# Two first loads change queues, and block 1's raw transposes go ahead of V of block 0

## The chip, the cores and the metric

The kernel runs on one core of a Trainium2 chip. A core has TensorE (PE, matrix products), VectorE (DVE), ScalarE (ACT), GpSimd (POOL) and SyncE (SP), which work side by side and wait for one another through semaphores. Loads and stores are DMAs; here SyncE, ScalarE and GpSimd issue them, each in its own queue, and the core's 16 DMA engines carry them out. The metric is the device time of one execution in microseconds (us).

## What is computed

The input x is 2048 rows of 512, in bfloat16. The result is the sum of x and two branches that both read the row-normalised x:

```python
xn = _layernorm(x, axis=-1)
return x + _A_ref(xn, A_wqkv, A_wo) + _B_ref(xn, B_w_in, B_w_sp, B_b_sp, B_w_out)
```

Branch A is attention with 32 heads of 16. Row s looks at the eight rows s, s-2, ..., s-14; Q, K and V come from one weight matrix of 512 x 1536, and a 512 x 512 matrix follows. Branch B multiplies xn by a 512 x 1792 matrix and takes GELU. It normalises the second half of the columns (z2), mixes it over all 2048 rows by a 2048 x 2048 matrix, adds a bias for each row, multiplies by the first half (z1), and projects back to 512 columns.

## The kernel before

**Tiling.** The rows are cut into 16 blocks of 128. Every matrix product needs x with the features on the partitions, so each block is transposed. Blocks 0 to 2 (`NRAW = 3`) are transposed raw by TensorE, against an identity matrix (`pe_tr`, L600): four matmuls of 128 columns a block, named xTx0a and xTx0b (two each), xTx1 and xTx2. ScalarE copies these from PSUM to SBUF (L628: xTc0_0, xTc0_1, xTc1_0, xTc1_1, xTc2_0). The product V of these blocks is made from the raw transposes, four matmuls of 512 columns a block, in two halves (V0_0, V0_1 and so on, L700). Each half reads the half of V's weights that it needs: `wv` half 0 (loaded by ldwv0) and half 1 (ldwv1), 256 KB each. Mean and scale are put right later. Beside this VectorE takes the statistics of each block (L620, L622, L632), GpSimd the inverse root (L634) and VectorE normalises (L646). Block 0's normalised rows are transposed by TensorE (xTr0, also L600, copied by ScalarE in L608), those of the later blocks by DMA (L640, named xTd1 and on, issued by SyncE). z2 is L831, Q and K are L723, z1 is L877, the mixing over rows L977, the two output products L1033 and L1042.

**Order.** Each operation is a task with engine, estimated time, reads and writes. `Plan.schedule` simulates the engines in the program's own time and fixes one static order for each engine; it uses estimates, and for some DMAs a landing time given in `land`. The eight banks of PSUM are given out as the simulation goes. Lists of names in `build_kernel` add edges that force an order; the longest is that of TensorE's first work. `Plan.emit` writes each engine's instructions with the waits that the order needs. An engine works strictly in its order, so an instruction that waits holds up all behind it.

**The first loads.** x of block b is 128 KB (`ld_x`, L535; ldx0 is written out in L562). ScalarE's queue issues ldx0 and ldx1 and then loads its activation table. SyncE's queue issues ldwv0, ldwv1, ldx2, ldx3, the two halves of z2's weights and more rows of x.

**The warm-up.** While nothing has landed, TensorE multiplies constants (`warm`, L581): warm0 to warm5 with 512 columns, warm6 with 128, and one more, warm7, with 128 columns, behind block 0's raw transposes.

Of the kernel before, what the change touches and what calls it, by code (L numbers as in the profile page):

```python
# [346 lines left out]
def build_kernel(nc, A_x, A_wqkv, A_wo, B_x, B_w_in, B_w_sp, B_b_sp, B_w_out, out, report=False, emit=True):  # L347
# [13 lines left out]
    NWARM = 7  # L361
# [8 lines left out]
    off = {}  # L370
# [40 lines left out]
    with ExitStack() as es:  # L411
# [5 lines left out]
        def A(name, n, o2_=0):  # L417
            return ar[:, off[name] + o2_: off[name] + o2_ + n]

        def AC(o_, dims):  # L420
            return bass.AP(tensor=ar, offset=o_, ap=[[AR, 128]] + [list(d) for d in dims])
# [10 lines left out]
        def P(bk, n, o_=0):  # L432
            return ps[:, bk.col(o_): bk.col(o_) + n]
# [78 lines left out]
        def dma(eng, fn, nbytes, chan, reads=(), writes=(), name="", xbar=False, prio=0.0, after=()):  # L512
            return T(eng, fn, reads=reads, writes=writes, name=name, prio=prio, after=after,
                     dma=dict(chan=chan, nbytes=nbytes, xbar=xbar, iss=(1270.0 if nbytes < 400000 else 2200.0) if xbar else None))
# [18 lines left out]
        def ld_x(b, eng="sp"):  # L533
            sl = b
            return dma(eng, lambda e: e.dma_start(A("xin", 512, 512 * sl), x2[128 * b:128 * b + 128, :]), 128 * 512 * 2,  # L535
                ("xin", sl), writes=[("xin", sl)], name="ldx%d" % b)

        def ld_wv(hf):
            dma("sp", lambda e: e.dma_start(AC(off["wv"] + 1024 * hf, [[512, 2], [1, 512]]),
                                            A_wqkv[256 * hf:256 * hf + 256, 1024:1536].rearrange("(c p) n -> p c n",  # L540
                                                                                               p=128)),
                256 * 512 * 2, ("wv", hf), writes=[("wv", hf)], name="ldwv%d" % hf)
# [13 lines left out]
        def ld_wqk(which, eng):  # L556
# [4 lines left out]

        dma("act", lambda e: e.dma_start(A("xin", 512), x2[0:128, :]), 128 * 512 * 2, ("xin", 0),  # L562
            writes=[("xin0", 0), ("xin0", 1)], name="ldx0")
        ld_x(1, "act")
        ld_wv(0)
        ld_wv(1)
        ld_x(2, "sp")
        ld_x(3, "sp")
        ld_win2a()
# [6 lines left out]
        ld_wqk(1, "sp")  # L576

        bw = plan.bank("warm")
        for wi in range(NWARM + 1):
            n_ = 512 if wi < 6 else 128  # L580
            T("pe", (lambda bw, n_: lambda t: t.matmul(P(bw, n_), ones[:, 0:128], ones[:, 0:n_], start=True,  # L581
                                                       stop=True))(bw, n_),
              writes=[bw], est=(427.0 if n_ == 512 else 107.0), name="warm%d" % wi, prio=1000)
# [487 lines left out]

        byname = {t.name: t for t in plan.tasks}
        for names in (["warm%d" % wi for wi in range(NWARM)] +
                      ["xTx0a", "xTx0b", "warm%d" % NWARM, "V0_0", "xTx1", "V0_1", "xTx2", "V1_0", "V1_1", "xTr0", "V2_0", "V2_1",
                       "z2_0_0", "z2_0_0b", "z2_0_1", "z2_1_0", "z2_1_1", "z2_2_0", "z2_2_1", "V3_0", "V3_1", "z2_3_0", "z2_3_1", "V4_0", "V4_1", "z2_4_0", "z2_4_1", "Q0_0", "Q0_1", "K0_0", "K0_1"],
                      ("rstd7", "Vw3"),
                      ("bnst0", "bnag0", "vpe0", "bnst1", "bnag1", "vpe1", "norm0", "bnst2", "norm1", "bnag2", "vpe2", "bnst3", "norm2",
                       "bnag3", "vpe3", "norm3", "bnst4", "bnag4", "vpe4", "mr", "norm4", "bnst5"),
                      ["bnst%d" % b for b in range(5, NB)],
                      ("xTc0_0", "xTc0_1", "xTc1_0", "xTc1_1", "xTc2_0", "xTe0_0", "xTe0_2", "Ve1", "Ve0", "Ve2",  # L1080
                       "z2g0", "z2g1", "z2s0"), ("ldx4", "xTd1", "xTd2", "xTd3", "xTd4", "ldq", "ldk", "ldx5", "ldx6", "ldx7", "ldwin1", "ldx8"), ("ldx15", "xTd5"),
                      *[("ldwin1", "ldx%d" % b) for b in range(9, NB)], *[("z2_4_1", "%s0_%d" % (n, c)) for n in "QK" for c in range(4)],
                      ("V10_1", "Q3_3"), ("csa", "csb", "csc", "csr", "ldwout"), ("csr", "ldwo0"), ("csr", "ldxr0"), ("csv", "zr3")):
            for n0, n1 in zip(names, names[1:]):
                if byname[n0] not in byname[n1].deps:
                    byname[n1].odeps.add(byname[n0])

        plan.schedule(tol=4.0, dma_bw=285.0, dma_lat=1600.0, overlap=60.0,
                      land=dict(ldx0=3600.0, ldwv0=4120.0, ldx1=4550.0, ldwv1=5230.0, ldx2=5600.0, ldwin2a=7650.0, ldx3=6050.0,
                                ldwin2b=8950.0, csa=75800.0, csb=78400.0, csc=83400.0, csr=86500.0, ldx4=9100.0, ldx5=18150.0, ldq=16300.0, xTd3=12130.0, ldk=17800.0, ldx6=18500.0, ldx7=18900.0, xTd4=13900.0, xTd1=9600.0, xTd2=10850.0, ldwin1=21500.0))  # L1090
        if report:
            print("arena", AR, "fp", FR)
# [17 lines left out]
def bass_parallel_sum__sliding_local_dilated__mixer_gmlp__prompt_kernel(  # L1110
    nc, A_x, A_wqkv, A_wo, B_x, B_w_in, B_w_sp, B_b_sp, B_w_out, out
):
    build_kernel(nc, A_x, A_wqkv, A_wo, B_x, B_w_in, B_w_sp, B_b_sp, B_w_out, out)
# [28 lines left out]
```

## Time and profile before

| | |
|---|---|
| median of 3 runs | 236.63 us (235.77 to 236.96) |
| the profiled execution | 236.54 us |
| its span, first to last instruction | 235.3 us |
| TensorE busy | 232.4 us, 99% |
| VectorE busy | 207.3 us, 88% |
| ScalarE busy | 95.9 us, 41% |
| data moved by DMA | 44.55 MB, mean 189 GB/s |

The span leaves out 1.2 us of the profiled execution's time. A line of the timeline gives the start and the length in us from the span's start, the engine, the line of the kernel, the operation with its output and input, the shapes, how many instructions are merged, and in brackets how long the engine was idle before and what ended that. A queue is named by its engine with a q behind it (SPq, ACTq). Matmuls are pipelined, so a matmul's length holds its drain, and the distance between starts says how fast TensorE streams. A line of the DMA issues gives the issuing queue, the number, the size and the time from issue to landing.

### The profile page before, as it was taken

To read this page: it belongs to the slowest core of one execution; us is meant where nothing else is said; L and a number is where in the kernel's file an instruction comes from. 1 tells how busy PE (TensorE), PEld (TensorE's weight loads), DVE (VectorE), ACT (ScalarE), POOL (GpSimd) and SP (SyncE) were. 2 spreads that over 40 slices of the span, in tenths; PEclk is the share of its full clock that TensorE was granted. 3 is DMA by queue.
4 is the path that set the end of the run, shared out by engine and by line. 5 is a ranking of instruction groups with operands and counts; after the bars stand their busy time and mean duration, and the time that the engine had idled before them with its cause. 6 is when DMAs were issued, how large, how long until landed. Compare 5 with 4: busy or idle time off the path is not lost.

```text
span 235.3 us, 3002 instructions
## 1 busy us (share of the span) xinstructions
PE 232.4 (99%) x1127; PEld 109.0 (46%) x1127; DVE 207.3 (88%) x271; ACT 95.9 (41%) x143; POOL 29.4 (12%) x58
## 2 busy tenths in 40 slices
PE   8999999999999999999999999999999999999996
PEld 3545445544454444444444444444444444444443
DVE  4706899999999999999899999998899998999723
ACT  3788878888986679610120531111111111000000
POOL 2305740404361202000000000000000000000000
PEclk9999999999999999999999999999999999999999
DMA  6669934999911285346199999999969849945442
GB/s 221 203 193 368 181 68 103 215 202 214 228 45 50 67 231 173 66 94 175 58 353 239 273 212 266 195 236 288 279 180 306 269 145 303 288 115 156 111 137 68
DMA packets 83991, 44.55 MB, mean 189 GB/s; under 512 B 56180, under 2 KB 83204, under 8 KB 83976
## 3 DMA queue, kind: packets, MB, share of 16 engines
q1 hardware_dynamic: 82744, 41.94, 69.6%
q0 software_dynamic: 800, 2.11, 3.0%
q10 hardware_dynamic: 432, 0.30, 0.4%
q8 instruction: 9, 0.15, 0.3%
q14 instruction: 6, 0.05, 0.1%
HBM read 26.62 MB, written 4.22 MB: 131 GB/s over the span
## 4 chain that ended last, share of the span: by engine, by line
PE 98%; DVE 0%; ACT 0%; issue 0%; DVEq 0%
PE ps L977 41%; PE ps L723 12%; PE ps L831 10%; PE ps L877 10%; PE ps L1042 10%; PE ps L700 6%; PE ps L1033 6%; PE ps L581 1%; PE ps L767 1%; PE ps L600 1%; DVE arena L1048 0%; ACT arena L628 0%; PE ps L778 0%; DVEq L325 0%
## 5 line engine op out<-in xcount | busy, mean ns | idle before, releaser
L977 PE MATMUL ps<-arena 128*128 128x512 bf16 x448 | 97.0, 379 | 0.0
L977 PEld LDWEIGHTS ps<-arena 128*128 128x128 bf16 x448 | 43.8, 98 | 53.0 <-issue 0.4
L985 ACT ACTIVATE arena<-ps 128x1024 bf16<-128x1024 f32 (+1 forms) x16 | 14.7, 917 | 77.0 <-PE ps L977 70.6
L1005 DVE TENSOR_TENSOR arena<-arena 128x4096 bf16<-128x4096 bf16 x16 | 36.4, 2282 | 0.0
L744 DVE TENSOR_TENSOR arena<-arena 128x4096 bf16<-128x4096 bf16 x16 | 36.4, 2280 | 0.0
L1008 DVE TENSOR_TENSOR arena<-arena 128x2048 bf16<-128x2048 bf16 (+1 forms) x32 | 30.0, 948 | 0.2
L723 PE MATMUL ps<-arena 128*128 128x512 bf16 x128 | 28.8, 379 | 0.0
L749 DVE TENSOR_TENSOR arena<-arena 128x4096 bf16<-128x4096 bf16 x12 | 27.4, 2287 | 0.1
L1042 PE MATMUL ps<-arena 128*128 128x512 bf16 (+2 forms) x119 | 27.0, 366 | 0.0
L831 PE MATMUL ps<-arena 128*128 128x448 bf16 x128 | 25.5, 352 | 0.0
L877 PE MATMUL ps<-arena 128*128 128x512 bf16 x112 | 24.5, 379 | 0.0
L723 PEld LDWEIGHTS ps<-arena 128*128 128x128 bf16 x128 | 14.4, 113 | 13.3 <-ACT arena L713 0.4
L732 ACT ACTIVATE arena<-ps 128x1024 bf16<-128x1024 f32 x16 | 16.2, 1022 | 6.8 <-PE ps L723 6.6
L1048 DVE TENSOR_TENSOR arena<-ps,arena 128x512 bf16<-128x512 f32 (+2 forms) x17 | 11.2, 656 | 8.6 <-PE ps L1042 8.5
L831 PEld LDWEIGHTS ps<-arena 128*128 128x128 bf16 x128 | 12.5, 98 | 12.1 <-issue 0.2
L1042 PEld LDWEIGHTS ps<-arena 128*128 128x128 bf16 x119 | 11.4, 98 | 12.9
L877 PEld LDWEIGHTS ps<-arena 128*128 128x128 bf16 x112 | 11.0, 98 | 13.2
L700 PE MATMUL ps<-arena 128*128 128x512 bf16 x64 | 16.8, 395 | 0.2 <-ACT arena L628 0.2
L1033 PE MATMUL ps<-arena 128*128 128x512 bf16 (+2 forms) x68 | 16.6, 366 | 0.0
L839 ACT ACTIVATE arena<-ps 128x896 bf16<-128x896 f32 x16 | 14.6, 913 | 3.4 <-PE ps L831 3.3
L883 ACT ACTIVATE arena<-ps 128x1024 bf16<-128x1024 f32 (+1 forms) x16 | 14.0, 919 | 4.4 <-PE ps L877 4.3
L620 DVE BATCH_NORM_STATS2 fpool<-arena 128x6 f32<-128x512 bf16 x16 | 10.7, 685 | 5.5 <-DMA arena<-in_A_x_dram 5.5
(64 smaller groups left out, 168.2 us busy)
## 6 DMA issues: line engine op xcount, KB each, us to landing
arena<-vscr SPq DMA_DIRECT2D x16, 1024.0 KB, 6.1
arena<-in_A_x_dram SPq DMA_DIRECT2D x30, 128.0 KB, 3.8
vscr<-arena POOLq DMA_DIRECT2D x16, 128.0 KB, 3.9
out_dram<-arena SPq DMA_DIRECT2D x15, 128.0 KB, 2.0
arena<-in_A_wqkv_dram SPq DMA_DIRECT2D x2, 512.0 KB, 4.6
arena<-in_B_w_in_dram SPq DMA_DIRECT2D x2, 448.0 KB, 4.9
arena<-in_B_w_in_dram SPq DMA_DIRECT2D x1, 896.0 KB, 8.2
arena<-in_B_w_out_dram SPq DMA_DIRECT2D x1, 896.0 KB, 5.9
```

The source lines that it names most:

```text
L700: last = t.matmul(P(bk, 512), A("xcT", 128, 512 * b + 128 * dc) if b < NRAW else xTv(b, dc), A("wv", 512, 512 * dc), start=(dc == 0), stop ...
L723: last = t.matmul(P(bk, 512, 512 * which), AC(off["wqk"] + 2048 * which + 512 * dc + c, [[4, 128]]), AC(off["xnT"] + dc * S + 512 * j, [[1 ...
L732: T("act", lambda a: a.activation(AC(qo, [[ko - qo, 2], [1, 512]]), P(bk, 1024).rearrange("p (t n) -> p t n", t=2), ACTF.Copy, scale=0.5), ...
L744: T("dve", (lambda pbv, qb, kb: lambda v: v.tensor_tensor(pbv, qb, kb, ALU.mult))(pbv, qb, kb), reads=rd, writes=[("pb", s_)], est=c_tt(40 ...
L749: T("dve", (lambda av, bv: lambda v: v.tensor_tensor(av, av, bv, ALU.add))(av, bv), reads=[("pb", 1)], writes=[("pb", acc)], est=c_tt(4096 ...
L831: last = t.matmul(P(bk, 448, 512 * hf), xTv(b, dc), AC(off["w_in2"] + 896 * dc + 448 * hf, [[1, 448]]), start=(dc == 0), stop=(dc == 3))
L877: last = t.matmul(P(bk, 512, 512 * i), AC(off["w_in1"] + 896 * dc + 128 * fc, [[1, 128]]), AC(off["xnT"] + dc * S + 512 * j, [[1, 512]]), ...
L977: last = t.matmul(P(bk, 512, 512 * i), AC(off["z2"] + FH * sh + 128 * fc, [[1, 128]]), AC(off["wT%d" % r_] + sh * 512, [[1, 512]]), start= ...
L1005: T("dve", lambda v: v.tensor_tensor(tv, tv, av, ALU.mult), reads=[("attn", b)], writes=[("Vs", sv)], est=c_tt(4096), name="pv%d" % b, pri ...
L1008: T("dve", (lambda n: lambda v: v.tensor_tensor(A("Vs", n, 4096 * sv), A("Vs", n, 4096 * sv), A("Vs", n, 4096 * sv + n), ALU.add))(n), wri ...
L1033: last = t.matmul(P(bk, cn), AC(off["OT"] + 512 * tb + 128 * cc, [[1, 128]]), AC(off["wo"] + 512 * cc + c0, [[1, cn]]), start=(cc == 0), s ...
L1042: last = t.matmul(P(bk, cn), AC(off["z1T"] + fc * S + 128 * tb, [[1, 128]]), AC(off["w_out"] + 512 * fc + c0, [[1, cn]]), start=False, sto ...
```

## The change

ldx1 is issued by SyncE as its first DMA, and ldwv0 by ScalarE as its second: the two change places. ldwv1 stays second on SyncE's queue. warm7 is no longer made. In TensorE's order xTx1 comes directly behind block 0's raw transposes, ahead of V0_0, and V0_0 and V0_1 follow one another. Two landing times that the planner is given are altered, those of the two DMAs.

```diff
-        def ld_wv(hf):
-            dma("sp", lambda e: e.dma_start(AC(off["wv"] + 1024 * hf, [[512, 2], [1, 512]]),
+        def ld_wv(hf, eng):
+            dma(eng, lambda e: e.dma_start(AC(off["wv"] + 1024 * hf, [[512, 2], [1, 512]]),
...
-        ld_x(1, "act")
-        ld_wv(0)
-        ld_wv(1)
+        ld_x(1, "sp")
+        ld_wv(0, "act")
+        ld_wv(1, "sp")
         ld_x(2, "sp")
         ld_x(3, "sp")
...
-        for wi in range(NWARM + 1):
+        for wi in range(NWARM):
...
-                      ["xTx0a", "xTx0b", "warm%d" % NWARM, "V0_0", "xTx1", "V0_1", "xTx2", "V1_0", "V1_1", "xTr0", "V2_0", "V2_1",
+                      ["xTx0a", "xTx0b", "xTx1", "V0_0", "V0_1", "xTx2", "V1_0", "V1_1", "xTr0", "V2_0", "V2_1",
...
-                      land=dict(ldx0=3600.0, ldwv0=4120.0, ldx1=4550.0, ldwv1=5230.0, ldx2=5600.0, ldwin2a=7650.0, ldx3=6050.0,
+                      land=dict(ldx0=3600.0, ldwv0=4450.0, ldx1=3800.0, ldwv1=5230.0, ldx2=5600.0, ldwin2a=7650.0, ldx3=6050.0,
```

## The prediction

> **What bounds the kernel now.** I read the page's busy times first, then the chain that ended last, then the start of the timeline on TensorE, ScalarE and the DMA queues, because the change lies wholly in the first 9 us. Sections 1 and 2 of the page:
>
> ```profile
> span 235.3 us, 3002 instructions
> ...
> PE 232.4 (99%) x1127; PEld 109.0 (46%) x1127; DVE 207.3 (88%) x271; ACT 95.9 (41%) x143; POOL 29.4 (12%) x58
> ...
> PE   8999999999999999999999999999999999999996
> DVE  4706899999999999999899999998899998999723
> ```
>
> TensorE works for 232.4 of 235.3 us. It has a hole only in the first and the last slice. The waits by engine, asked for TensorE alone, name two for the whole span:
>
> ```profile
> PE ps L581 <- PEq L1127: 0.8, 1, 0.8
> PE ps L700 <- ACT arena L628: 0.2, 1, 0.2
> ```
>
> So nothing after 9 us can be won except by less matmul work, and the change removes no useful matmul. What it can move is when TensorE reaches the back-to-back part. The timeline of the first microseconds (start, length, engine, line, shape, count), matmuls only:
>
> ```profile
> 0.84 2.83 PE L581 MATMUL ps<-const-bfloat16-1.0 128*128 128x512 bf16 x7 [0.84 <-PEq L1127]
> ...
> 3.62 0.61 PE L600 MATMUL ps<-arena 128*128 128x128 bf16 x4
> ...
> 4.02 0.31 PE L581 MATMUL ps<-const-bfloat16-1.0 128*128 128x128 bf16 x1
> 4.05 0.66 ACT L628 ACTIVATE arena<-ps 128x256 bf16<-128x256 f32 x2 [0.81 <-PE ps L600]
> ...
> 4.49 1.04 PE L700 MATMUL ps<-arena 128*128 128x512 bf16 x2 [0.16 <-ACT arena L628]
> ...
> 5.32 0.63 PE L600 MATMUL ps<-arena 128*128 128x128 bf16 x4
> ...
> 5.75 1.06 PE L700 MATMUL ps<-arena 128*128 128x512 bf16 x2
> ...
> 6.60 0.50 PE L600 MATMUL ps<-arena 128*128 128x128 bf16 x4
> ...
> 6.93 1.03 PE L700 MATMUL ps<-arena 128*128 128x512 bf16 x4
> ...
> 7.80 0.39 PE L600 MATMUL ps<-arena 128*128 128x128 bf16 x4
> ...
> 8.02 1.03 PE L700 MATMUL ps<-arena 128*128 128x512 bf16 x4
> ```
>
> Lengths hold the drain, so I use differences of starts. Block 0's transposes start at 3.62, warm7 at 4.02, V0_0 at 4.49, xTx1 at 5.32, V0_1 at 5.75, xTx2 at 6.60, V1 at 6.93, xTr0 at 7.80, V2 at 8.02. The reader is to see two rates. Up to xTx2 a 512-column matmul takes 0.427 us (5.75 to 6.60 for two) and a 128-column one 0.107 us (5.32 to 5.75 for four). From V1 on it is 0.216 us (6.93 to 7.80 for four) and 0.055 us. xTx2 took 0.33 us, which is two slow and two fast matmuls, so the step lies near 6.82 us. The column of granted clock shows 1.00 in every window of this stretch, so the step is seen in the spacing alone.
>
> The last view is the DMA issues by window, with the time from issue to landing:
>
> ```profile
> arena<-in_A_wqkv_dram SPq DMA_DIRECT2D x1, 256.0 KB, 3.3
> ...
> arena<-in_A_wqkv_dram SPq DMA_DIRECT2D x1, 256.0 KB, 3.9
> arena<-in_A_x_dram ACTq DMA_DIRECT2D x1, 128.0 KB, 3.3
> ```
>
> The first half of V's weights (ldwv0, SyncE, issued at 0.80) lands at 4.1; the second (ldwv1, 1.31) at 5.2; block 1's rows (ldx1, ScalarE, 1.25) at 4.55. Block 0's rows (0.81, 2.8 us) land at 3.6.
>
> **The change, part by part.**
>
> *The queues.* Both queues still issue as many DMAs as before: two on ScalarE (0.41 and 0.46 us), and on SyncE rows of x and weights of V at 0.45 to 0.46 us each. Nothing behind them moves: ScalarE's table load still starts at 1.74 and SyncE's third DMA at 1.82. Cost 0; what hides ScalarE's issue is the wait for block 0's transposes until 4.05, and without it one issue is 0.45 us, the same as before.
>
> *Block 1's rows* now start 0.45 us earlier at the head of SyncE's queue, where ldwv0 stood. They are 128 KB less than ldwv0, and at the 379 GB/s moved between 3.0 and 4.0 us that is 0.34 us: 4.1 - 0.34 = 3.76. The lower end is block 0's 3.6, the upper one 4.1. I take 3.8, before TensorE asks for it at 4.02.
>
> *V's first weights* now stand second on ScalarE's queue, at 1.25, where ldx1 stood. Ahead of them and with them go x0 and x1, so 512 KB are done when they are, as when ldx1 landed at 4.55. Lower end 4.1, their old landing. Upper end: the engines share evenly between the queues and ldwv1's 256 KB go along, 0.67 us more, 5.2, which is when all 768 KB are in today. I take 4.55: in the old run the second DMA of ScalarE's queue finished 0.65 us ahead of ldwv1, issued 0.06 us behind it, so it was not slowed to half rate. [...]
>
> *warm7 goes, xTx1 comes forward.* Today TensorE streams warm7 for 0.107 us at 4.02 and then stands 0.36 us until block 0's first evacuation (ACT L628, 0.38 us from 4.05) lets V0_0 go at 4.49. In the new order xTx1 takes 4.02 to 4.45 (four by 0.107). V0_0 then needs the evacuation (4.49, unchanged) and ldwv0 (4.55), so it starts at about 4.57, after a hole of 0.12 us. ScalarE runs block 1's evacuations about 0.9 us earlier, in time that was idle before (it waits 1.3 us for xTx1 today); no one stands behind them. If ldx1 were late, xTx1 would hold V0_0 back, since TensorE goes in order; at the upper end of 4.1 that is 0.1 us.
>
> *The sum.* V0 has four matmuls at 0.427, 1.71 us: 4.57 to 6.28. V0_1 starts at 5.42, after ldwv1's 5.2. xTx2 (x2 issued at 1.82, 3.8 us, so 5.6) goes from 6.28 to 6.71. V1 starts at 6.71 rather than 6.93; until the step at 6.82 it does a quarter of a matmul, the other 3.75 take 0.81 us: end 7.63 against 7.80. Gain 0.17 us. It is less than the half microsecond cleared at 4.0 because half of what is gained is slow time. At the ends: V0_0 at 4.49 (evacuation alone) gives xTr0 at 7.59, gain 0.21; V0_0 at 5.25 gives V0 until 6.96, of which 0.14 us lie behind the step and take 0.07, then xTx2 0.22 and V1 0.86: 7.97, a loss of 0.17.
>
> *Does the gain reach the end?* xTr0's input (normalised block 0, DVE L646 from 5.62 for 0.40) is there. The copy of xTx2 (0.60 us, today 7.13 to 7.73) ends near 7.45, and V2 asks at 7.85. xTr0's two copies (ACT L608, 8.22 today, 0.42 us behind xTr0's start, 0.33 each) come at 8.05, the first done at 8.38, and block 0's z2 (L831, 8.88 today) asks at 8.71. Block 1's transposed rows are issued at 6.96 and take 2.5 us, 9.46, against a use at 10.4, now 10.2. w_in1, issued at 15.66, lands at 23.9 against 25.1. The closest I found is 0.9 us, the second logits matmul at 119.1 behind an add that ended at 118.2. All exceed 0.17, so TensorE stays without holes and the tail follows its last matmul. The planner sees V0_1 wait for 5230 ns with either order, so I expect the same order on every engine behind it. Profiled execution: 236.54 - 0.17 = 236.37. It stands 0.09 us below the median of 236.63, so a median should be 236.4 to 236.5; I give 236.4.
>
> **The rivals.**
>
> *No gain (even sharing).* ldwv0 lands with ldwv1 near 5.2 and the hole before V0_0 becomes 0.8 us: 236.54 + 0.17 = 236.7. For it: from 3.0 us on the DMA engines are full (share 1.09 between 3.0 and 3.6). Against it: ldx1 today.
>
> *The change does not do what it says.* Block 1's rows land as late as 4.55 behind block 0's; xTx1 then runs 4.57 to 5.0 and V0_0 follows: V0 until 6.71, xTx2 until 6.94, V1 until 7.80, 236.5. For it: two transfers of x head both queues. Against it: ldwv0, twice as long, landed at 4.1 from that place.
>
> *Slower: the fast rate comes later.* It came 6.0 us after the first matmul at 0.84 and 2.3 us after the last hole ended at 4.49. If it hangs on unbroken work and the hole before V0_0 grows to 0.8 us, it comes at 5.25 + 2.3 = 7.55 at the least, or 5.25 + 6.0 = 11.25 at the most. Each microsecond later costs 1 - 0.216/0.427 = 0.49 us, so 0.36 to 2.2 on top of 0.17; half way 1.45, 238.0. It decides from a step 2.1 us later on. For it: the change takes a warm-up matmul away. Against it: a hole of 0.36 us did not stop the step, and the expected hole is 0.12. [...]
>
> *Faster: the fast rate comes earlier.* If today's hole held it back and the count runs from 0.84, 2.3 us are over before 3.62, and everything from there to 6.82 would go at twice the rate: 0.49 x 3.2 = 1.6, 234.8. Against it: the warm-up matmuls, 2.6 us on end from 0.84, did not bring it today.
>
> **How the numbers follow.** My forecast has 0.62, even sharing 0.19, the late rows 0.04: these three are within 0.5% (1.2 us, about what a measurement of this kernel can tell from no change, since its three runs span that much), 0.85. The late step has 0.09, slower; the early step 0.06, faster. The range runs from the fastest run shown less the best sum, 235.77 - 0.21 = 235.5, to the slowest plus the worst, 236.96 + 0.17 = 237.1. The two step rivals lie outside.
>
> **What would show it.** Right: xTx1 directly behind xTx0 near 4.02, V0_0 near 4.57, xTr0 near 7.63, no new wait of TensorE behind it. Wrong: a wait of L700 for A_wqkv beyond 0.3 us (landing), xTx1 waiting for x (rows), pairs of L700 matmuls still 0.85 us apart after 7.5 (step), or a hole behind 9 us (order).

## The result, and the profile after

The change made the kernel slower. Over 13 executions of each, the median is 238.0 us (236.05 to 238.41) with the change and 236.11 us (235.77 to 236.96) before. The ratio is 1.006, with a 95% interval from 1.0035 to 1.0085.

The 13 times do not lie around one value. Three are 236.05, 236.12 and 236.18; the other ten run from 237.18 to 238.41, eight of them from 237.96. The profiled execution is one of the three, 236.18 us, and so it is 0.36 us *shorter* than the profiled one of before. Whoever reads that profile alone sees the change as a gain:

```profile
span 234.9 us, 2980 instructions
...
PE 229.9 (98%) x1106; PEld 108.3 (46%) x1126; DVE 207.2 (88%) x271; ACT 95.8 (41%) x143; POOL 29.5 (13%) x58
```

TensorE is busy for 2.5 us less, but 1.1 us of that is no idle time: the trace has 1106 records of matmuls against 1127, one of them warm7, and small gaps stand behind 9 us where the other 20 are missing. The list of TensorE's waits names what is new, 1.2 us where 0.2 us stood before:

```profile
PE ps L700 <- DMA arena<-in_A_wqkv_dram: 1.2, 1, 1.2
```

The timeline of the changed kernel's first microseconds shows it in place:

```profile
3.54 0.72 PE L600 MATMUL ps<-arena 128*128 128x128 bf16 x8
...
5.42 1.02 PE L700 MATMUL ps<-arena 128*128 128x512 bf16 x4 [1.17 <-DMA arena<-in_A_wqkv_dram]
...
6.29 0.39 PE L600 MATMUL ps<-arena 128*128 128x128 bf16 x4
...
6.51 1.03 PE L700 MATMUL ps<-arena 128*128 128x512 bf16 x4
```

The eight raw transposes run on end from 3.54, as the new order asks. V0_0 then waits until 5.42, where it started at 4.49 before. But V0 goes at the full rate at once: four matmuls from 5.42 to 6.29, 0.217 us each. In this execution the step to the full rate came among the transposes, near 3.8 us, 3 us sooner than in the profile of before. The early step is worth more than the wait costs: z2's first matmul comes at 8.46 and not at 8.88, which explains the 0.4 us.

The DMA issues say why V0_0 waited. First the half that it needs, then the other:

```profile
arena<-in_A_wqkv_dram ACTq DMA_DIRECT2D x1, 256.0 KB, 4.1
arena<-in_A_wqkv_dram SPq DMA_DIRECT2D x1, 256.0 KB, 3.7
```

ldwv0, issued at 1.23, lands at 5.3; ldwv1, issued at 1.25 from the other queue, lands at 4.95. The stretch from 3.0 to 3.5 us adds a little. Its line gives busy times of the engines, the granted clock, the DMA share and the GB/s. With the change:

```profile
3.00:3.50 0.50, 0.50 (x3) 0.07 (x1) 0.00 (x0) 0.21 (x2) 0.00 (x0) 1.00 0.74 211
```

and before:

```profile
3.00:3.50 0.50, 0.50 (x3) 0.07 (x1) 0.00 (x0) 0.23 (x2) 0.00 (x0) 1.00 1.09 379
```

With two short transfers at the heads of the queues the DMA engines are less busy here (a share of 0.74 against 1.09). It is so in e6_half too, which has the same queues: 254 GB/s at a share of 0.84, against 379 to 381 GB/s at 1.09 to 1.10 in the kernel before, e7_order_fill and e8_before_fill, which have ldwv0 at a head. That the long ldwv0 covered this time is my reading of it; no run tests it. The profile explains the wait, but not the ten executions near 238, in which no profile of this kernel fell. That is what the runs are for.

### The profile page after: what moved, and what is told of

It is laid out like the page before. It is cut to its first block, busy times and chain, and to the rows that moved or that the text cites. A ratio compares the mean times of both kernels' runs of the same rounds, so it can differ in the third digit from the quotient of the medians.

```text
span 234.9 us, 2980 instructions
## 1 busy us (share of the span) xinstructions
PE 229.9 (98%) x1106; PEld 108.3 (46%) x1126; DVE 207.2 (88%) x271; ACT 95.8 (41%) x143; POOL 29.5 (13%) x58
## 4 chain that ended last, share of the span: by engine, by line
PE 96%; DMA 2%; issue 1%; ACTq 0%; DVE 0%
PE ps L977 41%; PE ps L723 12%; PE ps L831 10%; PE ps L877 10%; PE ps L1042 10%; PE ps L1033 6%; PE ps L700 6%; DMA arena<-in_A_wqkv_dram 2%; PE ps L767 1%; PE ps L600 0%; ACTq L562 0%; DVE arena L1048 0%; PE ps L778 0%
## 5 line engine op out<-in xcount | busy, mean ns | idle before, releaser
L977 PE MATMUL ps<-arena 128*128 128x512 bf16 x439 | 96.6, 379 | 0.5
L723 PE MATMUL ps<-arena 128*128 128x512 bf16 x124 | 28.2, 379 | 0.3 <-issue 0.2
L1042 PE MATMUL ps<-arena 128*128 128x512 bf16 (+2 forms) x116 | 26.5, 366 | 0.1
L877 PE MATMUL ps<-arena 128*128 128x512 bf16 x110 | 24.4, 379 | 0.1
L723 PEld LDWEIGHTS ps<-arena 128*128 128x128 bf16 x128 | 14.4, 114 | 13.3 <-ACT arena L713 0.4
L1033 PE MATMUL ps<-arena 128*128 128x512 bf16 (+2 forms) x68 | 16.6, 366 | 0.1
L700 PE MATMUL ps<-arena 128*128 128x512 bf16 x62 | 15.3, 379 | 1.3 <-DMA arena<-in_A_wqkv_dram 1.2
```

The costliest lines, as they stand in the source:

```text
L700: last = t.matmul(P(bk, 512), A("xcT", 128, 512 * b + 128 * dc) if b < NRAW else xTv(b, dc), A("wv", 512, 512 * dc), start=(dc == 0), stop ...
L723: last = t.matmul(P(bk, 512, 512 * which), AC(off["wqk"] + 2048 * which + 512 * dc + c, [[4, 128]]), AC(off["xnT"] + dc * S + 512 * j, [[1 ...
L877: last = t.matmul(P(bk, 512, 512 * i), AC(off["w_in1"] + 896 * dc + 128 * fc, [[1, 128]]), AC(off["xnT"] + dc * S + 512 * j, [[1, 512]]), ...
L977: last = t.matmul(P(bk, 512, 512 * i), AC(off["z2"] + FH * sh + 128 * fc, [[1, 128]]), AC(off["wT%d" % r_] + sh * 512, [[1, 512]]), start= ...
L1033: last = t.matmul(P(bk, cn), AC(off["OT"] + 512 * tb + 128 * cc, [[1, 128]]), AC(off["wo"] + 512 * cc + c0, [[1, cn]]), start=(cc == 0), s ...
L1042: last = t.matmul(P(bk, cn), AC(off["z1T"] + fc * S + 128 * tb, [[1, 128]]), AC(off["w_out"] + 512 * fc + c0, [[1, cn]]), start=False, sto ...
```

## The experiments

The theory: the hole ahead of V0_0 makes the step of TensorE's rate come a few microseconds later in most executions. The rivals: the late weights cost the time by the wait itself; or the new order of TensorE does. In each run "executions" are those of its own timing beside the kernel before on the same chip, whose medians were 236.18 us (e1 to e4), 235.90 (e5 to e8) and 236.01 (e9 to e11).

**The hole filled (e1_fill).** Eleven small matmuls on constants follow xTx1; everything else is the changed kernel (the planner is told 36 ns for each of the eleven).

```diff
-        for wi in range(NWARM):
+        for wi in range(NWARM + 11):
...
-                      ["xTx0a", "xTx0b", "xTx1", "V0_0", "V0_1",
+                      ["xTx0a", "xTx0b", "xTx1"] + ["warm%d" % wi for wi in range(NWARM, NWARM + 11)] + ["V0_0", "V0_1",
...
```

> The changed kernel with eleven 128-column matmuls on constants put between xTx1 and V0_0; queues and loads stay as changed, V0_0 still waits for ldwv0 until about 5.3. Theory (the hole of 1.3 us keeps TensorE at its slow rate for longer in most executions): with the hole filled (eleven by 0.107 us, to about 5.2) the slow cluster near 238 goes away, all executions between 235.9 and 236.9, median near 236.4. Rival (the late weights themselves cost the time, by the wait): the wait is unchanged, so still most executions near 238.

Median 236.55 us, from 236.29 to 236.91 in 11 executions; ratio to before 1.0018 (1.0009 to 1.0027). None lies near 238, though V0_0 started later still:

```profile
4.41 1.38 PE L581 MATMUL ps<-const-bfloat16-1.0 128*128 128x128 bf16 x11
5.89 1.25 PE L700 MATMUL ps<-arena 128*128 128x512 bf16 x4
6.98 0.39 PE L600 MATMUL ps<-arena 128*128 128x128 bf16 x4
```

V0 takes 1.09 us (5.89 to 6.98) where four slow matmuls would take 1.71: the step came near 6.4 us. The next run, on the same chip, has weights as late, no filling and TensorE's old order; its median is 1.4 us higher. So the wait as such is not the main cost: with the hole filled it costs 0.4 us.

**The queues alone (e2_queues).** TensorE's order and warm7 as before.

```diff
-        ld_x(1, "act")
-        ld_wv(0)
-        ld_wv(1)
+        ld_x(1, "sp")
+        ld_wv(0, "act")
+        ld_wv(1, "sp")
...
```

> The changed queues alone; TensorE's order as before, with warm7. V0_0 follows warm7 and waits for ldwv0. Theory: ldwv0 lands at 5.3, the hole before V0_0 is 1.2 us (4.1 to 5.35), and the executions fall into two clusters, one near 236.3 and most near 238, as with the whole change. Rival (the new order of TensorE is at fault): as before, median 236.1, all below 237.

Median 237.95 us, 1.0049 (1.0020 to 1.0078). Five of 12 executions lie from 236.34 to 236.75, seven from 237.91 to 238.76. The profiled one is of the upper group:

```profile
5.85 1.01 PE L700 MATMUL ps<-arena 128*128 128x512 bf16 x2 [1.47 <-DMA arena<-in_A_wqkv_dram]
6.66 0.63 PE L600 MATMUL ps<-arena 128*128 128x128 bf16 x4
7.08 1.06 PE L700 MATMUL ps<-arena 128*128 128x512 bf16 x2
...
8.36 1.47 PE L700 MATMUL ps<-arena 128*128 128x512 bf16 x4
9.66 0.39 PE L600 MATMUL ps<-arena 128*128 128x128 bf16 x4
```

From 6.66 to 7.08 four transposes still take 0.42 us; of the four matmuls of V1 (8.36 to 9.66) two are slow and two are fast. The step lies near 9.2 us, 2.4 us later than in the profile of before. The queues are enough for the whole effect, and this is the late step that no profile of the changed kernel caught.

**The order alone (e3_order).** Queues as before; xTx1 ahead of V0_0, no warm7.

```diff
-        for wi in range(NWARM + 1):
+        for wi in range(NWARM):
...
-                      ["xTx0a", "xTx0b", "warm%d" % NWARM, "V0_0", "xTx1", "V0_1", "xTx2",
+                      ["xTx0a", "xTx0b", "xTx1", "V0_0", "V0_1", "xTx2",
...
```

> The changed order of TensorE alone, without warm7; queues as before. xTx1 waits for ldx1, which lands at 4.55, so there is a hole of 0.45 us ahead of xTx1 and V0_0 starts near 5.0. Theory: a hole of that size lets the step come as it does before (0.36 us did), so nearly all executions between 235.8 and 237.0, median 236.3. Rival (the order is at fault): most near 238.

Median 236.01 us, 0.9998 (0.9986 to 1.0010): no difference. Eleven of 12 executions lie from 235.78 to 236.33, one at 237.5. The order is not at fault, and brings nothing either.

**A hole without a late load (e4_hole).** The kernel before with a shorter warm-up; TensorE idles before the first transposes and no load is touched.

```diff
-    NWARM = 7
+    NWARM = 4
...
-            n_ = 512 if wi < 6 else 128
+            n_ = 512 if wi < 4 else 128
```

> The kernel before, with only four of its six 512-column warm-up matmuls and none of warm6: TensorE stands idle from 2.55 to 3.6, all loads and V0_0's start at 4.49 stay. Theory (idle time in the first microseconds keeps the slow rate for longer): two clusters again, or all slower, most executions 1 to 2 us above the kernel before (237.2 to 238.4). Rival (only the wait for weights costs): as before, median 236.1, since nothing that the result needs is moved.

All six executions lie from 237.12 to 237.99, median 237.57, 1.0060 (1.0046 to 1.0073).

```profile
3.52 0.61 PE L600 MATMUL ps<-arena 128*128 128x128 bf16 x4 [0.82 <-DMA arena<-in_A_x_dram]
...
4.48 1.01 PE L700 MATMUL ps<-arena 128*128 128x512 bf16 x2 [0.24 <-ACT arena L628]
...
7.00 1.91 PE L700 MATMUL ps<-arena 128*128 128x512 bf16 x4
8.70 0.63 PE L600 MATMUL ps<-arena 128*128 128x128 bf16 x4
9.13 1.26 PE L700 MATMUL ps<-arena 128*128 128x512 bf16 x4
```

V0_0 starts at 4.48, as before, and nothing waits for weights. Yet V1 takes 1.70 us (7.00 to 8.70), the slow rate in full, where it took 0.87 before, and the step comes near 9.6. Idle time does it without a late load.

**Part of the hole filled (e6_half).** As e1_fill, with five in place of eleven.

> The changed kernel with five instead of eleven 128-column matmuls on constants between xTx1 and V0_0: 0.53 us of the hole filled, 0.4 to 0.8 us left. Theory (what counts is how much of the window before the step TensorE stands idle): between the two, so most executions from 236.1 to 237 and at most a few near 238. Rival (any hole longer than some tenths of a microsecond counts in full): two clusters as with the whole change, most near 238.

Median 236.45 us, 1.0022 (1.0006 to 1.0038). Eleven of 12 executions lie from 235.82 to 236.79, one at 238.16. How large a hole the other executions had is not known: in the profiled one, 235.96, ldwv0 landed at 5.1, TensorE's list has no wait there, and the step had come near 4.8, before V0. Few late steps are what the theory expected, but the rival, that any hole longer than some tenths counts in full, is not tested by so small a hole.

**Half as long an early hole (e10_hole5).** As e4_hole, with `NWARM = 5` and five 512-column matmuls.

> The kernel before with five of six 512-column warm-up matmuls and none of warm6: TensorE idle from 2.98 to about 3.6, so 0.5 us less idle time than with four; loads and V0_0's start stay. Theory (how much of the time before the step is idle decides): between the kernel before and the run with four, so two clusters, some executions near 236 and some above 237. Rival (any idle time there counts in full): all above 237, as with four.

Two executions at 236.7, four from 237.28 to 238.06; median 237.32, 1.0060 (1.0044 to 1.0077). Between the two, though nearer to e4_hole than I had thought: even the lower ones are above all 22 of the kernel before. The profiled one is of the lower pair, 236.69, with 0.4 and 0.2 us idle ahead of the first transposes and of V0_0:

```profile
6.61 0.55 PE L600 MATMUL ps<-arena 128*128 128x128 bf16 x4
...
7.00 1.03 PE L700 MATMUL ps<-arena 128*128 128x512 bf16 x4
```

Three of the four transposes of xTx2 are slow, so the step lies near 7.0.

**The change once more (e11_change).** The same kernel, on the chip of the next two.

> The changed kernel once more, beside the two others on the same chip. Theory: two clusters, a quarter to a half of the executions at 236.0 to 236.8 and the rest at 237.2 to 238.7; if the profiled one is of the slow cluster, its matmuls are still 0.427 us apart from V0_0 on and the step lies near 8 to 10 us. Rival (the 13 executions measured first were a chance of that chip): one cluster near 236.3.

Five of 11 executions from 236.09 to 236.73, one at 237.1, five from 237.76 to 238.45; median 237.1, 1.0051 (1.0027 to 1.0075). The profiled one, 236.4, had its step near 4.0 and a wait of 1.4 us for ldwv0, until 5.73.

**The halves of the weights exchanged (e9_swap).** The changed kernel, with ldwv0 second on SyncE's queue and ldwv1 second on ScalarE's.

```diff
-        ld_wv(0, "act")
-        ld_wv(1, "sp")
+        ld_wv(1, "act")
+        ld_wv(0, "sp")
```

> The changed kernel with the two halves of V's weights exchanged: ldwv0 second on SyncE's queue, ldwv1 second on ScalarE's. Same number and order of sizes on each queue. Theory (in this start the second transfer on SyncE's queue is served ahead of the second on ScalarE's, 4.95 against 5.33): ldwv0 lands near 4.95, V0_0 starts near 5.0, the hole is 0.4 us shorter than with the change, so fewer executions near 238 and the lowest ones near 235.9; ldwv1 at 5.3 is in time for V0_1 in the slow rate. Rival (ldwv0 is late by its size alone, both halves end together): ldwv0 lands at 5.3 again and the times are those of the change.

ldwv0, issued at 1.25, takes 3.9 us and lands at 5.13; ldwv1 lands 0.2 us behind it. So the second transfer of SyncE's queue indeed lands first, but by 0.2 and not 0.4 us. Eight of 12 executions lie from 235.78 to 236.50, four from 237.71 to 238.23; median 236.2, 1.0031 (1.0008 to 1.0055). The profiled one is of the upper group, with a hole of 0.46 us ahead of V0_0. The line names ScalarE's copies, the third of which ended at 5.23, but that is hardly what V0_0 waited for: in e5_sp3 it ran before the third copy had ended (4.84 against an estimated 4.93: ScalarE's copies end at 5.21 there, and in the change the third ends 0.28 us ahead of the fourth). It starts 0.13 us behind the landing of ldwv0, as it does in the change and in e1_fill, so the weights held it here too:

```profile
5.27 1.87 PE L700 MATMUL ps<-arena 128*128 128x512 bf16 x4 [0.46 <-ACT arena L628]
...
7.36 1.91 PE L700 MATMUL ps<-arena 128*128 128x512 bf16 x4
...
9.49 1.17 PE L700 MATMUL ps<-arena 128*128 128x512 bf16 x4
```

V0 and V1 are slow in full, V2 (9.49 to 10.49) in its first matmul; the step is near 9.8.

**ldwv0 behind ldx1 (e5_sp3).** ScalarE issues ldx0 alone; the rest is the changed kernel.

```diff
-        ld_wv(0, "act")
+        ld_wv(0, "sp")
```

> The changed kernel with ldwv0 on SyncE's queue, between ldx1 and ldwv1; ScalarE issues ldx0 alone. TensorE's order as changed. Theory (ldwv0 is late because it shares the DMA engines with ldwv1 from the other queue, both of 256 KB): with ldwv1 behind it in the same queue it lands at about 4.5, V0_0 starts near 4.6, the hole is 0.2 us at most, no execution lies in the cluster near 238, and the median is 0.1 to 0.3 us below the kernel before (236.0). [...]

A miss on all counts. ldwv0, issued at 1.25, takes 3.5 us: 4.75, earlier than 5.3 now that ldwv1 stands behind it and not beside it, but later than 4.5. SyncE now has one more issue ahead of z2's weights, and these made TensorE wait anew:

```profile
PE ps L831 <- DMA arena<-in_B_w_in_dram: 0.9, 2, 0.6
```

The halves of z2's weights, issued at 3.20 and 3.68, are there at 9.0 and 10.3, when TensorE goes on; in the kernel before the first was issued at 2.79 and landed at 7.3. Median 237.35 us, 1.0063 (1.0038 to 1.0087); the six executions run from 236.42 to 238.56. The profiled execution, 237.41, had its step near 5.7, so its loss is that wait and not the step. Whether the one at 238.56 had a late step is not known; the run decides nothing on late executions. Its profile does show that V0_0 ended a hole of 0.3 us at 4.84 and that the step came 0.8 us later:

```profile
4.84 1.43 PE L700 MATMUL ps<-arena 128*128 128x512 bf16 x4 [0.33 <-DMA arena<-in_A_wqkv_dram]
...
6.11 0.39 PE L600 MATMUL ps<-arena 128*128 128x128 bf16 x4
```

In e4_hole the last hole ended with V0_0 at 4.48, and the step came 5.1 us later. So the step does not follow the last hole by a fixed time, as it would if any hole started a count of unbroken work anew.

**Filling the holes that remain (e8_before_fill, e7_order_fill).** Four small matmuls take warm7's place in the kernel before, or stand ahead of xTx1 in e3_order.

> The kernel before with four 128-column matmuls on constants in place of warm7, so that the 0.36 us hole before V0_0 is filled. Theory: the few executions in which even that hole held the step back go (the kernel before had one at 238.49 in 29); the median stays near 236.1, none above 237. Rival (a shorter hole makes the step earlier in every execution): the median falls by 0.2 us or more.

Median 235.95 us, 235.78 to 236.26 in 11, ratio 1.0005 (0.9997 to 1.0014): no execution above 237, and no gain. The kernel before has one execution above 237 in the 93 that were timed.

> Queues as before, the changed order of TensorE, and four 128-column matmuls on constants between xTx0b and xTx1, so that the wait for ldx1 (4.02 to 4.49) is filled. Theory: as with the order alone (median near 236.0), but no execution above 237; the order alone had one at 237.5 in twelve. Rival (the one at 237.5 has another cause): now and then one above 237 all the same.

Median 236.35 us, 235.77 to 236.66 in 11, ratio 1.0013 (1.0003 to 1.0022). None above 237, as expected; that the median lies 0.3 us above what I expected is not explained.

The runs together, by TensorE's waits between the warm-up and V0 as the waits by engine list them (of one profiled execution each; e5_sp3 is left out for its other loss; e4_hole's and e10_hole5's are two waits added):

| kernel | TensorE idle there | executions above 237 |
|---|---|---|
| e1_fill, e7_order_fill, e8_before_fill | none listed | 0 of 33 |
| e6_half | none listed | 1 of 12 |
| before | 0.2 us | 1 of 93 |
| e3_order | 0.3 us | 1 of 12 |
| e9_swap | 0.5 us | 4 of 12 |
| e10_hole5 | 0.7 us | 4 of 6 |
| e4_hole | 1.1 us | 6 of 6 |
| the change, both times | 1.2 and 1.4 us | 16 of 24 |
| e2_queues | 1.5 us | 7 of 12 |

The late executions become many between 0.3 and 0.5 us. Above that the counts do not rise in step: 1.1 us, most of it ahead of the first transposes, made all six executions late; 1.2 to 1.5 us ahead of V0 made 23 of 36 late. Whether the place of the hole matters, or this is chance, was not tried.

No version beat the kernel before.

## Why the prediction was wrong

*What held.* Nothing behind 9 us changed: the order of all engines behind the first loads and V0 is the same. The one new entry in TensorE's list of waits there, 0.2 us at 72.27 (L723), stands where the trace lacks records of matmuls (it has 124 of that line's 128); the traces of all the runs have the same gap. The issues cost nothing (table load at 1.72, before 1.74). Block 1's rows came even earlier than the 3.8 I took: issued at 0.80, landed at 3.3, 2.5 us later. xTx1 ran directly behind xTx0, and e3_order shows that the new order does no harm.

*The step that failed first* is "I take 4.55" for the landing of ldwv0. It was 5.3, just past the upper end of my bounds (5.2), and from 5.1 to 5.75 in the four other profiles with these queues. My reason was that ldx1 in the old run had come 0.65 us ahead of ldwv1 from the same place. That carried a 128 KB transfer's time over to one of 256 KB that competes with its equal. In all six profiles of this start, e9_swap's with the halves exchanged among them, SyncE's second transfer even landed first, by 0.2 to 0.4 us. The first half came when the last of the 768 KB were in, as the rival of even sharing had it; how the DMA engines divided their time between the queues, no view shows. With it fell "starts at about 4.57, after a hole of 0.12 us": it was 5.42, and the profile shows 1.17 us idle.

*The step that cost the time* is that the sum, and the rival of even sharing, took the step of the rate as fixed at 6.82 us. That rival had the landing right and its price, +0.17 us, wrong. The rival "the fast rate comes later" had the place right (the hole before V0_0). Its sign, slow pairs of V after 7.5 us, is seen in e2_queues, which has the same queues. Its time, 238.0 forecast and 238.0 measured as the median, is right in part by luck: it was the middle between two counts of unbroken work (2.3 and 6.0 us), and the runs show no such count (the step came 0.8 us behind V0_0's start in e5_sp3 and 5.1 us in e4_hole). I gave it 0.09 because I saw it as a second mishap on top of the first. It is a consequence of the first: with a hole of 1.2 to 1.4 us 16 of 24 executions lay above 237, with 0.5 us (e9_swap) 4 of 12, so its chance hung on that of even sharing. "A hole of 0.36 us did not stop the step" was true, and says nothing of one of 1.2.

*The step's price.* In the profiles of before, the change (twice) and the runs, the step lies between 3.8 and 7.0 us in ten (in e7_order_fill and e8_before_fill by an estimate from the chain that ended last, in which z2's matmuls begin near 8.1 and 8.4 us, against 8.88 in the kernel before), and between 9.2 and 9.8 in three (e2_queues, e4_hole, e9_swap); in none it lies between. Two profiles show what a later step costs, as V0_0 starts at 4.48 and 4.53 in them: e4_hole, step near 9.6, took 237.96 us, and e10_hole5, step near 7.0, took 236.69. That is 1.27 us for 2.6, or 0.49 us for each microsecond, as the prediction had it. In e2_queues wait and step add up to the loss: V0_0 starts 1.36 us later than before, in time at the slow rate, which costs half, 0.7 us, and the step 2.4 us later costs 1.2. The sum is 1.9, and so is the difference of the profiled executions (238.43 and 236.54).

Why idle time delays the step is not shown. The granted clock reads 1.00 for every profiled execution, and in the kernel before also from 6.6 to 6.8 and from 6.8 to 7.0 us, on both sides of the step at 6.82; only the spacing of the matmuls shows it. What the runs show is that idle time delays the step: in e4_hole, with 0.8 us ahead of the first transposes and no load touched, it came near 9.6.

*The range* had the kernel's own spread, 235.5 to 237.1, and left out both rivals that move the step; ten of the 13 executions lie above it.

## What to carry to other kernels

When TensorE's first microseconds decide, ask of every wait how much idle time it adds before the rate steps up, and price the late step as well as the wait: here a wait of more than 1 us cost 0.4 us where it was filled with work on constants, and about 2 us in most executions where it was not. Two transfers of equal size at the same place in two queues landed within 0.4 us of each other here, so do not expect the one beside to be early. In e5_sp3 the first half, put ahead of the other in one queue, landed 0.6 us sooner, but z2's weights behind it were late. And one profile can be of the lucky kind: read the list of all times before the trace.

## What the runs showed of the hardware

I had not expected so sharp an effect of idle time: with 1.1 us idle up to V0 (e4_hole) all six executions were late, with 0.2 us (the kernel before) one in 93. Nor had I expected the start of the DMA queues to be so tight: with 128 KB at both heads and the two halves of V's weights second (the change) the DMA engines moved 211 GB/s from 3.0 to 3.5 us against 379 with 256 KB at one head (the kernel before), and with one more issue ahead of z2's weights on SyncE (e5_sp3) the first half landed 1.7 us later than in the kernel before, though it was issued only 0.4 us later. Why it was so much more than the issue itself was not tried.
